# Edge columns of the filter loaded elsewhere, and small butterfly operations joined

## The chip, the cores and the metric

The kernel runs on one core of a Trainium2 chip. The metric is the device time of one execution in microseconds (us). The core's engines are TensorE (PE: matmuls; PEld its weight loads), VectorE (DVE), ScalarE (ACT), GpSimd (POOL) and SyncE (SP, which here only issues transfers); each runs its own list of instructions in order and waits for the others by semaphores. SP, ACT and POOL each have a queue of DMA transfers.

## The reference

```python
def _A_ref(x, w_r, w_i):
    X = jnp.fft.rfft2(x, axes=(-2, -1))
    X = X * (w_r + 1j * w_i)
    return jnp.fft.irfft2(X, s=(S, D), axes=(-2, -1))

def _B_ref(x, w1, w2):
    h = _silu(jnp.einsum("bsd,df->bsf", x, w1))
    return jnp.einsum("bsf,fd->bsd", h, w2)

xn = _layernorm(x, axis=-1)
s = _A_ref(xn, A_w_r, A_w_i)
g = _silu(_B_ref(xn, B_w1, B_w2))
return x + s * g
```

x is 2048 x 1024 (S x D), all in float32; w1 is 1024 x 3584, w2 3584 x 1024, and the filter w_r, w_i 2048 x 513 each.

## The kernel before

**Numbers.** Every operand of a matmul is split into a high and a low fp16 part, and a product is three matmuls (high-high, high-low, low-high). The high part is written by ACT (a copy with rounding), the low one by DVE (value minus high part, scalar_tensor_tensor at L230). The parts of the second matmul's operands travel through DRAM: hd_one, hd_sum and their like are stored on POOL's queue (L463) and loaded back as ht; w2's pieces are stored as ws and loaded back as jr (L387), then made into w by ACT (L227) and DVE (L230).

**The three streams of PE.** PE's list is written out ahead of time. First come 112 steps of the first matmul (h = xn w1, 24 matmuls of 128x512 each, L431). Then come 56 groups of the second matmul, pbM_J with M = 0 to 6 (seven products of a Strassen scheme over 2x2 blocks) and J = 0 to 7 (token tiles); a group is 42 matmuls (L509 to L511); the last one, pb6_7, is cut into two halves of half width. Between these stand, as a third stream in the background, the steps of the spectral part: layernorm, the forward transform (fa, then a butterfly on DVE at L757 to L790), the filter, the edge columns, and the inverse transform.

**The filter (f_gen, L883 to L1028)** runs in 16 steps u, beside the groups pb0_0 to pb2_x. A step loads vq (the forward result) and wq (four loads of the filter's columns) on SP's queue, multiplies on PE (fx, L914 to L916), forms X on DVE, scales wq on ACT (L997), multiplies X by wq on DVE (T, L1002), forms Z, and splits Z into the high and the low part of zq, in pieces by residue class (by_class, L937): ACT writes the high part (L954), DVE the low one (L960). Four steps fill one zq tile, which POOL's queue stores (zd, L965); the tile has a single buffer, so ACT's first piece of the next four waits for the stores. Each step also put two loads of the filter's edge columns (xsv, 64 x 4 elements of 4 bytes) on SP's queue (L987 to L989), delayed by a few steps (defer). edge_gen (L1030) uses them after the filter.

**The inverse transform (i_gen, L1122)** runs once per c, in the order 1, 3, 0, 2 (IORDER), beside groups pb2_x to pb6_x. At its start DVE copies the edge column into zt (L1129); PE's iu matmuls read zt. Then post (uw, ub, ud) and split make us on DVE and ACT, PE's id matmuls read us, and bfly (sw, st, spq, sab, so, s) makes the result s, which SP stores as sd. An output tile is the sum of a group's product and earlier ones (pl, kept), a silu on ACT (L590), and times s plus x on DVE (L583, L584), then a store.

**What sets the order.** While the list is written, `work()` (L1327) puts a background step behind a matmul step or group only while DVE's clock is not ahead of PE's by more than LEAD = 1:

```python
COST = {"DVE": ("dve", 0.07, 1.045e-3), "PE": ("pe", 0.0025, 0.4167e-3)}
...
clock["dve"] = max(clock["dve"], clock["pe"] - 1.0)
for _ in range(3):
    if clock["dve"] > clock["pe"] + LEAD or hold[0] or slot(bg) == PAUSE:
        break
```

Each DVE instruction moves DVE's clock by a fixed part and a part per element (meter, L189). So the number of DVE instructions decides where background steps stand on every engine's list.

Of the kernel before, what the change touches and what calls it, by code (L numbers as in the profile page):

```python
# [13 lines left out]
OP = mybir.AluOpType  # L14
# [90 lines left out]
def spectral_ffn(ctx, tc, x, w_r, w_i, w1, w2, ca, kc, ci, tw, pm, out):  # L105
# [648 lines left out]
    def fd_gen(c):  # L754
# [3 lines left out]
        def bfly(p):  # L758
# [12 lines left out]
            ds = ap.tile([128, 2, 2, 65], F32, name=f"DS{c}_{p}", tag="DS", bufs=1)  # L771
            tt(ds[:, 0], o[:, 1], o[:, 3], op=OP.subtract)
            tt(ds[:, 1], o[:, 1], o[:, 3], op=OP.add)
            pp = ap.tile([128, 4, 65], F32, name=f"P{c}_{p}", tag="P", bufs=1)
            tt(pp[:, 0:4:3], o[:, 0], o[:, 2, ::-1], op=OP.add)
            tt(pp[:, 2:0:-1], o[:, 0], o[:, 2, ::-1], op=OP.subtract)
            qq = ap.tile([128, 4, 65], F32, name=f"Q{c}_{p}", tag="Q", bufs=1)
            tt(qq[:, 0:4:3], ds[:, 0], ds[:, 1, ::-1], op=OP.add)
            tt(qq[:, 2:0:-1], ds[:, 0], ds[:, 1, ::-1], op=OP.subtract)
# [103 lines left out]
    def f_gen():  # L883
# [53 lines left out]
        def by_class(u):  # L937

            j = u % 4
            zv = zs_[u].rearrange("m n (i h l) -> m n h l i", h=2, l=8)  # L940
            qv = [zqs[u // 4][:, k].rearrange("m (n g b) i -> m n b g i", g=4, b=4)[:, :, :, :, 8 * j:8 * j + 8] for k in range(2)]
            first = [v[:, :, :, 0].rearrange("m n (l h) i -> m n h l i", h=2) for v in qv]
            for z, o in ((zv[:, :, :, 1:4], [v[:, :, 0:4:3, 3:0:-1] for v in qv]),
                         (zv[:, :, :, 5:8], [v[:, :, 2:0:-1, 1:4] for v in qv]),
                         (zv[:, :, :, 0:8:4], first)):
                yield z, o

        def high_z(u):
# [21 lines left out]
        for u in range(16):  # L970
# [56 lines left out]
        yield 1  # L1027

# [93 lines left out]
    def i_gen(c):  # L1122
# [21 lines left out]
        def post(g):  # L1144
# [4 lines left out]
            b = ip.tile([128, 2, 2, 128], F32, name=f"ub{c}_{g}", tag="ub", bufs=1)  # L1149
            d = ip.tile([128, 2, 2, 128], F32, name=f"ud{c}_{g}", tag="ud", bufs=1)  # L1150
# [37 lines left out]
        def bfly(p):  # L1188
# [110 lines left out]
    with tc.manual_schedule():  # L1299
# [79 lines left out]
        for n, (c, f) in enumerate(order):  # L1379
# [125 lines left out]
```

## Time and profile before

| what | us |
|---|---|
| median of 3 runs (1285.46, 1286.04, 1294.56) | 1286.04 |
| the profiled execution | 1284.65 |
| its span (first to last instruction) | 1282.9 |
| PE busy in it | 1234.2 (96%) |
| DVE busy | 1033.5 (81%) |
| ACT busy | 501.5 (39%) |
| POOL busy | 243.0 (19%) |

The span is the time from the first to the last instruction in the profiled execution; what lies around it is 1284.65 - 1282.9 = 1.75 us. TensorE's granted clock, as a mean over the span, was 0.985 of full speed. PE is the engine that is busy nearly throughout; the rows below tell where it is not. The lines of code are those of the kernel before.

### The profile page before, as it was taken

To read this page: it belongs to the slowest core of one execution; us is meant where nothing else is said; L and a number is where in the kernel's file an instruction comes from. 1 tells how busy PE (TensorE), PEld (TensorE's weight loads), DVE (VectorE), ACT (ScalarE), POOL (GpSimd) and SP (SyncE) were. 2 spreads that over 40 slices of the span, in tenths; PEclk is the share of its full clock that TensorE was granted. 3 is DMA by queue.
4 is the path that set the end of the run, shared out by engine and by line. 5 is a ranking of instruction groups with operands and counts; after the bars stand their busy time and mean duration, and the time that the engine had idled before them with its cause. 6 is when DMAs were issued, how large, how long until landed. Compare 5 with 4: busy or idle time off the path is not lost. (4 is left out here: it accounts for less than half of the span.)

```text
span 1282.9 us, 20862 instructions
## 1 busy us (share of the span) xinstructions
PE 1234.2 (96%) x7759; PEld 624.8 (49%) x7759; DVE 1033.5 (81%) x2284; ACT 501.5 (39%) x684; POOL 243.0 (19%) x389
## 2 busy tenths in 40 slices
PE   8998999999999999999999797999999998999996
PEld 5544455445445444445455454544554544455543
DVE  7688898998998997648957998872695896896897
ACT  4865344334365455436443443331122321332211
POOL 1231231222243344231221000013012010000000
PEclk9999999999999999999999798999999999999998
DMA  7477376565487779585876977877579599697688
GB/s 236 135 179 184 99 251 174 174 198 165 156 255 252 251 256 327 176 287 165 183 261 219 236 233 194 256 264 280 170 202 277 203 343 343 224 355 278 224 307 285
DMA packets 175735, 296.90 MB, mean 231 GB/s; under 512 B 39696, under 2 KB 92688, under 8 KB 175120
## 3 DMA queue, kind: packets, MB, share of 16 engines
q1 hardware_dynamic: 133232, 161.25, 41.1%
q0 software_dynamic: 26560, 82.86, 21.0%
q10 hardware_dynamic: 15840, 51.45, 11.6%
q8 instruction: 61, 1.00, 0.3%
q14 instruction: 42, 0.34, 0.1%
HBM read 186.97 MB, written 104.33 MB: 227 GB/s over the span
## 5 line engine op out<-in xcount | busy, mean ns | idle before, releaser
L431 PE MATMUL pa<-xnT,w 128*128 128x512 f16 x2688 | 586.7, 380 | 6.8 <-DMA xnT<-xs 4.4
L431 PEld LDWEIGHTS <-w 128*128 128x128 f16 x2688 | 262.6, 98 | 319.0 <-issue 7.7
L509 PE MATMUL pb<-w,ht 128*128 128x512 f16 (+1 forms) x798 | 301.6, 378 | 3.2 <-DMA ht<-hd_sum_d 3.2
L510 PE MATMUL pb<-w,ht 128*128 128x512 f16 (+1 forms) x798 | 301.0, 377 | 0.0
L511 PE MATMUL pb<-w,ht 128*128 128x512 f16 (+1 forms) x798 | 300.6, 377 | 0.0
L509 PEld LDWEIGHTS <-ht 128*128 128x128 f16 x798 | 78.4, 98 | 93.9 <-DMA ht<-hd_sum_d 3.4
L511 PEld LDWEIGHTS <-ht 128*128 128x128 f16 x798 | 78.4, 98 | 92.4 <-issue 2.1
L510 PEld LDWEIGHTS <-ht 128*128 128x128 f16 x798 | 78.4, 98 | 87.6 <-issue 1.3
L440 ACT ACTIVATE h<-pa,s 128x512 f32<-128x512 f32 x112 | 75.7, 676 | 104.2 <-PE pa L431 103.7
L227 ACT ACTIVATE w<-jr,sc 128x512 f16<-128x512 f32 x98 | 68.7, 713 | 108.0 <-DMA jr<-in_B_w_dram 82.2
L230 DVE SCALAR_TENSOR_TENSOR w<-jr,sc,w 128x512 f16<-128x512 f32 x98 | 71.6, 745 | 18.2 <-ACT w L227 18.2
L463 POOL DMA_DIRECT2D hd_sum<-hosum x52 | 38.0, 765 | 230.2 <-DVE hosum L230 115.2
L227 ACT ACTIVATE hoone<-h,hs 128x2048 f16<-128x2048 f32 x28 | 56.0, 1999 | 55.5 <-DMA hd_one<-hoone 26.0
L230 DVE SCALAR_TENSOR_TENSOR hoone<-h,hs,hoone 128x2048 f16<-128x2048 f32 x28 | 65.6, 2343 | 12.6 <-ACT hoone L227 12.6
L227 ACT ACTIVATE hosum<-hr,hs 128x1536 f16<-128x1536 f32 x28 | 44.0, 1572 | 76.5 <-DVE hr L470 61.3
L954 ACT ACTIVATE zq<-Z 128x192 f16<-128x192 f32 (+1 forms) x96 | 38.7, 483 | 79.3 <-DVE Z L217 58.9
L469 DVE TENSOR_TENSOR hr<-h 128x1024 f32<-128x1024 f32 x28 | 34.1, 1219 | 36.3 <-ACT h L440 36.2
L914 PE MATMUL fx<-vq,kq 128*128 128x256 f16 x192 | 47.8, 291 | 15.8 <-DMA vq<-vd 9.0
L463 POOL DMA_DIRECT2D hd_one<-hoone x52 | 45.2, 869 | 69.5 <-DVE hoone L230 24.2
L391 POOL DMA_DIRECT2D jr<-in_B_w_dram x28 | 24.6, 1018 | 171.1 <-DMA jr<-in_B_w_dram 35.3
L230 DVE SCALAR_TENSOR_TENSOR hosum<-hr,hs,hosum 128x1536 f16<-128x1536 f32 x28 | 50.7, 1810 | 4.7 <-ACT hosum L227 4.7
L227 ACT ACTIVATE w<-w1r,rs 128x1024 f16<-128x1024 f32 x28 | 32.0, 1145 | 49.8 <-DVE rs L258 22.4
(215 smaller groups left out, 1725.3 us busy)
## 6 DMA issues: line engine op xcount, KB each, us to landing
w1r<-in_B_w_dram SPq DMA_DIRECT2D x28, 512.0 KB, 5.8
w2m<-in_B_w_dram SPq DMA_DIRECT2D x28, 512.0 KB, 6.5
ht<-hd_dif ACTq DMA_DIRECT2D x32, 448.0 KB, 6.7
jr<-in_B_w_dram SPq DMA_DIRECT2D x56, 256.0 KB, 6.9
ht<-hd_sum ACTq DMA_DIRECT2D x32, 448.0 KB, 5.3
ht<-hd_one ACTq DMA_DIRECT2D x32, 448.0 KB, 6.7
hd_sum<-hosum POOLq DMA_DIRECT2D x52, 256.0 KB, 3.6
hd_one<-hoone POOLq DMA_DIRECT2D x52, 256.0 KB, 5.2
```

Of the source, the lines that this page charges most:

```text
L227: nc.scalar.activation(hi, raw, AF.Copy, scale=scale)
L230: nc.vector.scalar_tensor_tensor(lo, raw, scale, hi, op0=OP.mult, op1=OP.subtract)
L391: nc.gpsimd.dma_start(raw[n], w2_block(*todo[n], 1), accum_op=OP.add)
L431: nc.tensor.matmul(ps, w[:, wh, d], xt[:, xh, d], start=(n == 0), stop=(n == 23))
L440: nc.scalar.activation(hq[:, 2 * (c % 2) + f % 2], ps, AF.Silu, scale=s1[:, f:f + 1])
L463: defer(1, lambda k=k, m=m: stores[0].dma_start(hd[m, g][:, :, q].rearrange("f p h s -> f p (h s)"), o[:, k].rearrange("f p h s -> f p (h ...
L469: tt(sums[:, 0:2], hq[:, 0::2], hq[:, 1::2], op=OP.subtract)
L509: nc.tensor.matmul(ps, hh[:, 0], w[:, 0], start=first, stop=False)
L510: nc.tensor.matmul(ps, hh[:, 0], w[:, 1], start=False, stop=False)
L511: nc.tensor.matmul(ps, hh[:, 1], w[:, 0], start=False, stop=last)
L914: nc.tensor.matmul(o, k[:, c, kh, 1], v[:, c, vh], start=(n == 0), stop=False)
L954: nc.scalar.activation(o[0][:, :, h], z[:, :, h], AF.Copy)
```

## The change

In the filter, the two edge loads of each step leave SP's queue. A new function, load_edge, issues the same 32 loads on POOL's queue, one at each of the steps 44 to 75 of the first matmul. The classes of zq are written in five pieces in place of six, in another order of the 16 residues inside zq and zt. On DVE, operations on neighbouring tiles are written as one with a wider access pattern: in the forward butterfly P and Q are halves of one tile PQ, in post ub and ud halves of one tile, in bfly pairs of the last sums. DVE has 2062 instructions in place of 2286, ACT 752 in place of 768, SP 497 in place of 529, POOL 428 in place of 396. PE's are the same in number. The diff, cut to its core (bfly's first part and the common lines are left out):

```diff
@@ -768,15 +768,12 @@
...
-            ds = ap.tile([128, 2, 2, 65], F32, name=f"DS{c}_{p}", tag="DS", bufs=1)
-            tt(ds[:, 0], o[:, 1], o[:, 3], op=OP.subtract)
-            tt(ds[:, 1], o[:, 1], o[:, 3], op=OP.add)
-            pp = ap.tile([128, 4, 65], F32, name=f"P{c}_{p}", tag="P", bufs=1)
-            tt(pp[:, 0:4:3], o[:, 0], o[:, 2, ::-1], op=OP.add)
-            tt(pp[:, 2:0:-1], o[:, 0], o[:, 2, ::-1], op=OP.subtract)
-            qq = ap.tile([128, 4, 65], F32, name=f"Q{c}_{p}", tag="Q", bufs=1)
-            tt(qq[:, 0:4:3], ds[:, 0], ds[:, 1, ::-1], op=OP.add)
-            tt(qq[:, 2:0:-1], ds[:, 0], ds[:, 1, ::-1], op=OP.subtract)
+            tt(t0[:, 0], o[:, 1], o[:, 3], op=OP.subtract)
+            tt(t0[:, 1], o[:, 1], o[:, 3], op=OP.add)
+            pq = ap.tile([128, 2, 4, 65], F32, name=f"PQ{c}_{p}", tag="PQ", bufs=1)
+            pp, qq = pq[:, 0], pq[:, 1]
+            tt(pq[:, :, 0:4:3], t0[:, 4::-4], t0[:, 6::-5, ::-1], op=OP.add)
+            tt(pq[:, :, 2:0:-1], t0[:, 4::-4], t0[:, 6::-5, ::-1], op=OP.subtract)
...
@@ -937,27 +934,24 @@
...
-            zv = zs_[u].rearrange("m n (i h l) -> m n h l i", h=2, l=8)
-            qv = [zqs[u // 4][:, k].rearrange("m (n g b) i -> m n b g i", g=4, b=4)[:, :, :, :, 8 * j:8 * j + 8] for k in range(2)]
-            first = [v[:, :, :, 0].rearrange("m n (l h) i -> m n h l i", h=2) for v in qv]
-            for z, o in ((zv[:, :, :, 1:4], [v[:, :, 0:4:3, 3:0:-1] for v in qv]),
-                         (zv[:, :, :, 5:8], [v[:, :, 2:0:-1, 1:4] for v in qv]),
-                         (zv[:, :, :, 0:8:4], first)):
-                yield z, o
+            zv = zs_[u].rearrange("m n (i l) -> m n l i", l=16)
+            qv = [zqs[u // 4][:, k].rearrange("m (n l) i -> m n l i", l=16)[:, :, :, 8 * j:8 * j + 8] for k in range(2)]
+            for first, n, to, by in ((1, 3, 0, 4), (4, 4, 14, -4), (9, 4, 3, 4), (13, 3, 9, -4)):
+                stop = to + by * (n - 1) + (1 if by > 0 else -1)
+                yield zv[:, :, first:first + n], [v[:, :, to:stop if stop >= 0 else None:by] for v in qv]
+            yield zv[:, :, 0:9:8], [v[:, :, 12:14] for v in qv]
...
             for z, o in by_class(u):
-                for h in range(2):
-                    nc.scalar.activation(o[0][:, :, h], z[:, :, h], AF.Copy)
+                nc.scalar.activation(o[0], z, AF.Copy)
...
             for z, o in by_class(u):
-                for h in range(2):
-                    nc.vector.tensor_tensor(o[1][:, :, h], z[:, :, h], o[0][:, :, h], op=OP.subtract)
+                nc.vector.tensor_tensor(o[1], z, o[0], op=OP.subtract)
...
@@ -984,9 +978,6 @@
...
-            i_, n_, q_ = u // 8, u // 4 % 2, u % 4
-            for b in range(2):
-                defer(3, lambda i_=i_, n_=n_, q_=q_, b=b: nc.sync.dma_start(xsv[64 * b:64 * b + 64, 1 + n_, q_, :, i_:i_ + 1], wv[i_][q_][b, :, :, 512 * n_:512 * n_ + 1]))
...
@@ -1026,6 +1017,11 @@
...
+    def load_edge(k):
+        n_, b, q_ = k // 4 % 2, k // 8 % 2, k % 4
+        i_ = k // 16
+        nc.gpsimd.dma_start(xsv[64 * b:64 * b + 64, 1 + n_, q_, :, i_:i_ + 1], wv[i_][q_][b, :, :, 512 * n_:512 * n_ + 1])
...
@@ -1126,7 +1122,7 @@
...
-        nc.vector.tensor_copy(zt[:, :, :, :, 0, 0], zp[:, c])
+        nc.vector.tensor_copy(zt[:, :, :, :, 12, 0], zp[:, c])
...
@@ -1136,7 +1132,7 @@
...
-                            lhs = zt[rows_, q, zh, r, 4 * g:4 * g + 4].rearrange("m l i -> m (l i)")
+                            lhs = zt[rows_, q, zh, r, 12 - 4 * g:16 - 4 * g].rearrange("m l i -> m (l i)")
...
@@ -1146,22 +1142,20 @@
...
-            b = ip.tile([128, 2, 2, 128], F32, name=f"ub{c}_{g}", tag="ub", bufs=1)
-            d = ip.tile([128, 2, 2, 128], F32, name=f"ud{c}_{g}", tag="ud", bufs=1)
+            bd = ip.tile([128, 2, 2, 2, 128], F32, name=f"ub{c}_{g}", tag="ub", bufs=1)
+            b, d = bd[:, 0], bd[:, 1, :, ::-1]
...
-            tt(bv[:, 0], sums[:, 0:2], sums[:, 2:4], op=OP.add)
-            tt(dv[:, 0], sums[:, 0:2], sums[:, 2:4], op=OP.subtract)
-            for j, x_, y_ in ((0, dif[:, 0], dif[:, 2, ::-1]), (1, turn[:, 0:2, 0], turn[:, 2:4, 0])):
-                tt(bv[:, 1, j, 0], x_[:, 0], y_[:, 0], op=OP.subtract)
-                tt(dv[:, 1, j, 1], x_[:, 1], y_[:, 1], op=OP.subtract)
-                tt(dv[:, 1, j, 0], x_[:, 0], y_[:, 0], op=OP.add)
-                tt(bv[:, 1, j, 1], x_[:, 1], y_[:, 1], op=OP.add)
...
+            tt(b[:, :, :, 0:64], sums[:, 0:2], sums[:, 2:4], op=OP.add)
+            tt(d[:, :, :, 0:64], sums[:, 0:2], sums[:, 2:4], op=OP.subtract)
+            x_ = w[:, 1:3, 0].rearrange("m j k a -> m k j a")
+            y_ = w[:, 1:3, 2, ::-1].rearrange("m j k a -> m k j a")
+            tt(bd[:, :, :, 0, 64:128], x_, y_, op=OP.subtract)
+            tt(bd[:, ::-1, :, 1, 64:128], x_, y_, op=OP.add)
...
@@ -1210,21 +1204,16 @@
...
-            tt(s_[:, 0], pc, u, op=OP.add)
-            tt(s_[:, 4], pc, u, op=OP.subtract)
-            tt(s_[:, 2], pm_, v, op=OP.subtract)
-            tt(s_[:, 6], pm_, v, op=OP.add)
-            stt(s_[:, 1], o12[:, 0], RH, qm, op0=OP.mult, op1=OP.add)
-            stt(s_[:, 5], o12[:, 0], -RH, qm, op0=OP.mult, op1=OP.add)
-            stt(s_[:, 7], o12[:, 1], RH, qp, op0=OP.mult, op1=OP.add)
-            stt(s_[:, 3], o12[:, 1], -RH, qp, op0=OP.mult, op1=OP.add)
+            tt(s_[:, 0:7:6], pq[:, :, 0], ab[:, :, 0], op=OP.add)
+            tt(s_[:, 4:1:-2], pq[:, :, 0], ab[:, :, 0], op=OP.subtract)
+            stt(s_[:, 1:8:6], o12, RH, pq[:, ::-1, 1], op0=OP.mult, op1=OP.add)
+            stt(s_[:, 5:2:-2], o12, -RH, pq[:, ::-1, 1], op0=OP.mult, op1=OP.add)
...
@@ -1398,6 +1387,8 @@
...
             chunks[0] = sum(last_use[k] < n for k in range(4))
+            if 44 <= n < 76:
+                load_edge(n - 44)
...
```

The order of the lists moves with the count. Three places follow. The first is SP's queue in the filter stage, around the load of vq8. Of the kernel before (jr28 is a piece of w2, wq7 the filter's columns for step 7):

```order
L387 DMA jr27_6652<-ws1_13_164 128x512
L387 DMA jr28_6726<-ws2_0_165 128x512
L387 DMA jr29_6736<-ws2_1_166 128x512
L989 DMA xsv_215<-in_A_w_r_dram 64x4x1 x2
L902 DMA wq7_0_6770<-in_A_w_r_dram 64x4x128 x2
L902 DMA wq7_1_6773<-in_A_w_i_dram 64x4x128 x2
L387 DMA jr30_6776<-ws2_2_167 128x512
L894 DMA vq8_6787<-vd0_75 128x2048
```

Of the changed kernel:

```order
L387 DMA jr27_6601<-ws1_13_164 128x512
L387 DMA jr28_6680<-ws2_0_165 128x512
L891 DMA vq8_6691<-vd0_75 128x2048
L387 DMA jr29_6707<-ws2_1_166 128x512
L899 DMA wq7_0_6739<-in_A_w_r_dram 64x4x128 x2
L899 DMA wq7_1_6742<-in_A_w_i_dram 64x4x128 x2
L387 DMA jr30_6745<-ws2_2_167 128x512
```

The edge loads are gone, and vq8 stands behind jr28, where before it stood behind jr30.

The second is DVE's list where the inverse transform of c = 0 begins (zt0 is the copy that PE's iu0 waits for; pl4_3 and pl4_4 are the additions behind the groups pb4_3 and pb4_4; w2_5 is a low part of w2's pieces). Before:

```order
L557 TENSOR_TENSOR pl4_3_1_10787<-pl4_3_1_10787,pb4_3_10761 128x512
L558 TENSOR_TENSOR pl4_3_0_10789<-pl4_3_0_10789,pb4_3_10761 128x512
L230 SCALAR_TENSOR_TENSOR w2_5_1_10645<-jr83_10716,sc2_228,w2_5_1_10645 128x512
L583 SCALAR_TENSOR_TENSOR pl4_3_1_10787<-fs1_3_0_10819,s_sc_218,pl4_3_1_10787 128x512
L584 TENSOR_TENSOR pl4_3_1_10787<-pl4_3_1_10787,fx1_3_0_10821 128x512
L557 TENSOR_TENSOR pl4_4_1_10863<-pl4_4_1_10863,pb4_4_10837 128x512
L558 TENSOR_TENSOR pl4_4_0_10865<-pl4_4_0_10865,pb4_4_10837 128x512
L1129 COPY zt0_10199<-zp_214 128x16
L1151 TENSOR_TENSOR uw0_0_11057<-iu0_0_10959,uw0_0_11057 128x512
```

Changed:

```order
L557 TENSOR_TENSOR pl4_3_1_10596<-pl4_3_1_10596,pb4_3_10570 128x512
L558 TENSOR_TENSOR pl4_3_0_10598<-pl4_3_0_10598,pb4_3_10570 128x512
L230 SCALAR_TENSOR_TENSOR w2_5_1_10485<-jr83_10556,sc2_228,w2_5_1_10485 128x512
L1125 COPY zt0_10000<-zp_214 128x16
L1147 TENSOR_TENSOR uw0_0_10803<-iu0_0_10705,uw0_0_10803 128x512
```

The copy moved up, from behind the additions of group pb4_4 to behind the w2 piece that follows those of pb4_3. On PE's list iu0 moved from behind pb4_5 to behind pb4_4; iu3 likewise moved from the middle of pb3_5 to behind pb3_4 (its copy from behind the kept addition of group 4 to the w2 piece behind that of group 3), iu2 from behind pb5_6 to behind pb5_5, id3 from the middle of pb4_0 to behind pb3_7, id0 from behind pb5_1 to the middle of pb5_0, and id2 from the middle of pb6_2 to behind pb6_0.

The third is DVE's list at the end, from the last instruction of the last butterfly (s2_3). Before:

```order
L1227 SCALAR_TENSOR_TENSOR s2_3_13193<-so2_3_13192,spq2_3_13186 128x128
L583 SCALAR_TENSOR_TENSOR pl6_3_2_12985<-fs0_3_1_13013,s_sc_218,pl6_3_2_12985 128x512
L584 TENSOR_TENSOR pl6_3_2_12985<-pl6_3_2_12985,fx0_3_1_13015 128x512
L583 SCALAR_TENSOR_TENSOR pl6_3_0_12987<-fs0_3_0_13017,s_sc_218,pl6_3_0_12987 128x512
L584 TENSOR_TENSOR pl6_3_0_12987<-pl6_3_0_12987,fx0_3_0_13019 128x512
L569 TENSOR_TENSOR pl6_4_2_13135<-pl6_4_2_13135,pb6_4_13107 128x512
L570 TENSOR_TENSOR pl6_4_0_13137<-pl6_4_0_13137,pb6_4_13107 128x512
```

Changed:

```order
L1216 SCALAR_TENSOR_TENSOR s2_3_12771<-so2_3_12770,spq2_3_12764 128x2x128
L583 SCALAR_TENSOR_TENSOR pl6_1_2_12494<-fs0_1_1_12596,s_sc_218,pl6_1_2_12494 128x512
L584 TENSOR_TENSOR pl6_1_2_12494<-pl6_1_2_12494,fx0_1_1_12598 128x512
L583 SCALAR_TENSOR_TENSOR pl6_1_0_12496<-fs0_1_0_12600,s_sc_218,pl6_1_0_12496 128x512
L584 TENSOR_TENSOR pl6_1_0_12496<-pl6_1_0_12496,fx0_1_0_12602 128x512
L569 TENSOR_TENSOR pl6_2_2_12714<-pl6_2_2_12714,pb6_2_12686 128x512
L570 TENSOR_TENSOR pl6_2_0_12716<-pl6_2_0_12716,pb6_2_12686 128x512
```

The last butterfly now ends ahead of the outputs of group pb6_1; before it ended ahead of those of pb6_3.

## Rows read from the trace of the kernel before

**Rows 1.** The page, part 1: busy time, share and instructions.

```profile
PE 1234.2 (96%) x7759; PEld 624.8 (49%) x7759; DVE 1033.5 (81%) x2284; ACT 501.5 (39%) x684; POOL 243.0 (19%) x389
```

**Rows 2.** PE's waits: engine, line, releaser: us in total, times, longest.

```profile
PE fx L914 <- DMA vq<-vd: 9.0, 1, 9.0
PE fx L914 <- DMA jr<-ws: 6.8, 1, 6.8
...
PE pb L509 <- DMA ht<-hd_sum_d: 3.2, 1, 3.2
```

**Rows 3.** Stretches: length, busy of PE, PEld, DVE, ACT, POOL, clock, DMA, GB/s.

```profile
240.00:400.00 160.00, 160.00 (x873) 78.27 (x872) 150.83 (x313) 73.02 (x86) 49.17 (x69) 1.00 0.66 207
690.00:860.00 170.00, 149.37 (x879) 81.01 (x877) 150.41 (x292) 68.80 (x140) 11.09 (x26) 0.93 0.81 238
```

**Rows 4.** The same table for two short stretches.

```profile
719.00:729.00 10.00, 5.63 (x38) 4.65 (x39) 9.93 (x19) 3.00 (x8) 0.00 (x0) 0.50 0.90 291
1080.00:1086.00 6.00, 3.23 (x99) 2.90 (x100) 1.79 (x4) 1.32 (x2) 0.00 (x0) 1.00 0.91 301
```

**Rows 5.** Timelines of SP, ACT and DVE, 676 to 692 us: start, length, work, idle.

```profile
676.53 1.27 SPq L989 DMA_DIRECT2D xsv<-in_A_w_r_dram  x2
677.89 4.22 SPq L902 DMA_DIRECT2D wq<-in_A_w_r_dram  x2
...
689.02 0.72 ACT L227 ACTIVATE w<-jr,sc 128x512 f16<-128x512 f32 x1 [8.04 <-DMA wq<-in_A_w_r_dram]
...
681.22 2.17 DVE L960 TENSOR_TENSOR zq<-Z,zq 128x192 f16<-128x192 f32 x6
690.39 1.22 DVE L1002 TENSOR_TENSOR T<-X,wq 128x1024 f32<-128x1024 f32 x1 [7.00 <-ACT wq L997]
```

**Rows 6.** Waits of ACT and of DVE, 655 to 860 us.

```profile
ACT zq L954 <- DMA zd<-zq: 20.4, 3, 10.5
...
DVE T L1002 <- ACT wq L997: 14.0, 6, 7.0
```

**Rows 7.** Timeline of DVE in a last butterfly, 1130 to 1132 us.

```profile
1130.36 0.21 DVE L1200 SCALAR_TENSOR_TENSOR sw<-sw,st 128x64 f32<-128x64 f32 x1
1130.49 0.21 DVE L1201 SCALAR_TENSOR_TENSOR sw<-sw,st 128x64 f32<-128x64 f32 x1
...
1131.15 0.42 DVE L1210 TENSOR_TENSOR spq<-sw 128x256 f32<-128x256 f32 x1
1131.49 0.42 DVE L1211 TENSOR_TENSOR spq<-sw 128x256 f32<-128x256 f32 x1
```

**Rows 8.** The page, part 5: a group of instructions on POOL.

```profile
L463 POOL DMA_DIRECT2D hd_sum<-hosum x52 | 38.0, 765 | 230.2 <-DVE hosum L230 115.2
```

**Rows 9.** Timelines of PE and DVE around two starts of the inverse transform (iu).

```profile
983.66 0.38 PE L510 MATMUL pb<-w,ht 128*128 128x512 f16 x1
...
989.70 0.38 PE L511 MATMUL pb<-w,ht 128*128 128x512 f16 x1
...
1082.77 0.40 PE L1141 MATMUL iu<-kk,zt 64*128 64x128 f16 x8 [3.55 <-DVE zt L1129]
...
989.85 0.20 DVE L1129 COPY zt<-zp 128x16 f16<-128x16 f16 x1
...
1075.57 0.75 DVE L230 SCALAR_TENSOR_TENSOR w<-jr,sc,w 128x512 f16<-128x512 f32 x1 [1.37 <-ACT w L227]
...
1081.91 0.69 DVE L558 TENSOR_TENSOR pl<-pl,pb 128x512 f32<-128x512 f32 x1 [2.61 <-DMA pl<-pd]
```

**Rows 10.** Timelines of PE, SP and DVE at the end.

```profile
1270.33 0.27 PE L511 MATMUL pb<-w,ht 128*128 128x256 f16 x1
...
1267.20 0.32 SPq L502 DMA_DIRECT2D pl<-pd  x1
...
1271.83 0.42 DVE L569 TENSOR_TENSOR pl<-pl,pb 128x256 f32<-128x256 f32 x1 [4.63 <-DMA fs<-sd]
...
1277.21 0.41 DVE L569 TENSOR_TENSOR pl<-pl,pb 128x256 f32<-128x256 f32 x1
```

More of the change, by code (lines that the diff above doesn't have):

```diff
@@ L1154, in post @@
             nc.vector.tensor_single_scalar(dif[:, 1:4:2], dif[:, 1:4:2], RH, op=OP.mult)
-            tt(turn[:, 0:4:3, 0], dif[:, 1:4:2, 0], dif[:, 1:4:2, 1], op=OP.subtract)
-            tt(turn[:, 1:3, 0], dif[:, 1:4:2, 0], dif[:, 1:4:2, 1], op=OP.add)
-            bv, dv = (v.rearrange("m c r (e a) -> m e c r a", e=2) for v in (b, d))
-            tt(bv[:, 0], sums[:, 0:2], sums[:, 2:4], op=OP.add)
-            tt(dv[:, 0], sums[:, 0:2], sums[:, 2:4], op=OP.subtract)
-            for j, x_, y_ in ((0, dif[:, 0], dif[:, 2, ::-1]), (1, turn[:, 0:2, 0], turn[:, 2:4, 0])):
-                tt(bv[:, 1, j, 0], x_[:, 0], y_[:, 0], op=OP.subtract)
-                tt(dv[:, 1, j, 1], x_[:, 1], y_[:, 1], op=OP.subtract)
-                tt(dv[:, 1, j, 0], x_[:, 0], y_[:, 0], op=OP.add)
-                tt(bv[:, 1, j, 1], x_[:, 1], y_[:, 1], op=OP.add)
+            tt(turn[:, 0:3:2, 0], dif[:, 1:4:2, 0], dif[:, 1:4:2, 1], op=OP.subtract)
+            tt(turn[:, 0:3:2, 1], dif[:, 1:4:2, 0], dif[:, 1:4:2, 1], op=OP.add)
+            tt(b[:, :, :, 0:64], sums[:, 0:2], sums[:, 2:4], op=OP.add)
[4 more added lines that the diff above has]
+            tt(bd[:, ::-1, :, 1, 64:128], x_, y_, op=OP.add)
             u = ip.tile([128, 8, 128], F32, name=f"uu{c}_{g}", tag="s", bufs=2)
@@ L1199, in bfly @@
             stt(o1[:, 0], d1[:, 1], -S16, t_[:, 2, 0], op0=OP.mult, op1=OP.add)
-            stt(o1[:, 1], d1[:, 0], S16, t_[:, 2, 1], op0=OP.mult, op1=OP.add)
+            wd, wo, tf = (v.rearrange("s g r d -> s (g r) d") for v in (w[:, 1], w[:, 2], t_))
+            stt(wo[:, 3:8:4], wd[:, 3:7:3], S16, tf[:, 0:6:5], op0=OP.mult, op1=OP.add)
             stt(o3[:, 0], d3[:, 0], S16, t_[:, 0, 1], op0=OP.mult, op1=OP.subtract)
-            stt(o3[:, 1], d3[:, 1], S16, t_[:, 0, 0], op0=OP.mult, op1=OP.add)
             tt(o2[:, 0], t_[:, 1, 0], t_[:, 1, 1], op=OP.subtract)
@@ L1212, in bfly @@
             tt(abv[:, 0], y1, y3, op=OP.add)
-            tt(abv[:, 1], y1, y3, op=OP.subtract)
-            pc, qp, pm_, qm = pq[:, 0, 0], pq[:, 0, 1], pq[:, 1, 0], pq[:, 1, 1]
-            u, t_, r, v = ab[:, 0, 0], ab[:, 0, 1], ab[:, 1, 0], ab[:, 1, 1]
+            tt(abv[:, 1, ::-1], y1, y3, op=OP.subtract)
+            t_, r = ab[:, 0, 1], ab[:, 1, 1]
             o12 = ip.tile([128, 2, 128], F32, name=f"so{c}_{p}", tag="so", bufs=1)
```

## The prediction

> **What bounds the kernel now.** I read the engines' shares first. TensorE (PE) is busy 1234.2 of 1282.9 us [rows 1], so a faster VectorE (DVE) pays only where PE waits for it, and behind PE's last matmul. Next the list of PE's waits: 9.0 + 6.8 us stand at the filter's matmuls (fx) and 3.2 us at the second matmul's operand (ht) [rows 2]; the inverse transform's (iu) stands under [rows 9]. Then the table of stretches: in 690 to 860 us PE works 149.37 of 170 us, idle 20.6, at a mean granted clock of 0.93, while DVE is busy 150.41 [rows 3]. The clock comes on top of each stall: from 719 to 729 us, around the second stall, PE's 5.63 busy us ran at 0.50, the lower of its two levels [rows 4], 2.8 us lost; at the stage's mean of 0.93 the loss is at most 0.07 x 149 = 10.5 us. So this stage holds up to 31 us, and the end another 12.3: the last matmul begins at 1270.33 us and lasts 0.27 [rows 10], and the span ends at 1282.9. The rest of PE's time is matmuls, whose number the change leaves alone.
>
> **The DVE instructions.** It removes 224 of DVE's 2286 instructions and no element: 32 in the forward butterfly, 96 in the inverse one, 80 in the last (sw), 16 in the filter's classes. The price of one is read from starts: operations of 64 elements follow each other every 0.135 us, of 256 every 0.34 [rows 7]; the slope is 0.205/192 = 1.07 ns an element, and 0.135 - 64 x 0.00107 = 0.067 us is left for the instruction. 224 x 0.067 = 15 us of DVE. Most lies beside PE work and is worth nothing by itself; per inverse butterfly pair (a post and a sw) it is 11 x 0.067 = 0.74 us. The new operands keep runs of 64 or 65 contiguous elements, so I keep that slope. The filter's pieces do not: their inputs stand 64 bytes apart, as before. Six pieces, of 171 elements on the mean, take 2.17 us [rows 5], 0.36 each or 2.1 ns an element, so five save one instruction, 0.07 us a step, 1.1 us in all. The Trainium skill (SBUF — State Buffer, the note on cachelines) says that consecutive accesses pay when each falls into a new 16-byte line; the longer time per element of these pieces agrees with it, and by it joining them cannot bring the 1.07 ns.
>
> **The edge loads.** 32 loads of 64x4x1 elements leave SP's queue in the filter stage. A pair costs SP 1.27 us [rows 5], 16 pairs 20 us. The place that shows most: such a pair was issued at 676.53 us, and the next two filter loads (wq) then took SP 4.22 us; ACT stood 8.0 us for these loads, and DVE, with nothing else to do, 7.00 until 690.39 [rows 5]. That idle stretch ends in PE's ht and fx stalls some 15 to 30 us later. In 655 to 860 us DVE waits 14.0 us for ACT's scaling of wq [rows 6], 7.0 of it here. With the pair gone, and step 8's operand (vq8) in the queue ahead of the w2 pieces 29 and 30 and of four wq loads that it stood behind, I take that 7.00 as gained. Gains stop there: ACT also waits 20.4 us, three times, for the zq stores (single buffer), the longest 10.5 [rows 6], and stores are not made faster; and DVE's own work fills 88% of the stage. PE gets no more than DVE's chain gains. Bounds: 2 us, if the stores take back what is gained; 16, if all of DVE's 14.0 and its 1.1 return, with a us of clock. Inside I take **-7**, by the one pair that the trace shows.
>
> On POOL's queue the loads come one for each of 32 first-matmul steps, at about 235 to 400 us. POOL is busy 49.17 of 160 us in 240 to 400 [rows 3]; a store's issue there costs 0.765 us [rows 8], so 24 us more; even at twice that POOL stays below its 160. PE is busy 160.00 of those 160 us [rows 3], and each store waits at most one load longer. I cost this at **0**; the cover is that the edge values are read only at the end of the filter stage and the hd stores have 300 us. If the cover fails, ACT waits for hd buffers and PE for ACT. The Trainium skill (DMA: Bandwidth & Descriptors, SWDGE vs HWDGE vs iDMA) says that GpSimd writes its descriptors into rings in SBUF that DVE locks it out of in its 2-port mode, and that SP's DMAs are immune: by it this move goes the wrong way. The trace doesn't bear it out at this size: with DVE busy 150.83 of 160 us the stores' mean issue is 0.765 us [rows 3, 8].
>
> **The order that moves.** The planner meters DVE by instruction, so cheaper butterflies put inverse steps earlier on PE's list. Their condition, the zt copy on DVE, moves less. iu3 comes half a group earlier, and a group is 42 matmuls, whose starts lie 0.216 us apart (28 steps from 983.66 to 989.70), 9.1 us: PE asks at 985.4 rather than right after the matmul at 989.70. The copy, at 989.85 behind group 4's addition, loses only that one addition of 0.6 us [rows 9]; it would come at 989.2 and, with DVE running earlier, about 1.3 sooner. New stall 2.5, within 0 to 3.8: **+2.5**. iu0 comes a whole group earlier, 1070 rather than 1079; the copy moves from behind group 4's addition, which waited for a transfer (1081.91), to behind group 3's and one w piece (1075.57 + 0.7) [rows 9]. Stall 6.2 instead of 3.55: **+2.6**, between -3.5 (w comes early) and +5.5. Of the clock I add 0.4 for both: the stall before iu0 cost none, since the granted clock stood at 1.00 through 1080 to 1086 [rows 4].
>
> **The end.** The last butterfly (sw of tile 3) moves from behind group 6_3 to behind 6_1, two groups earlier, and DVE has only output work behind it. Before, that butterfly and the outputs queued behind it kept the pl loads of the last group, whose buffers come free late, from being issued until 1267.20, and its addition waited 4.63 us, to 1271.83 [rows 10]. Without the backlog the first half of the last group is ready at about 1266.0 (4.6 us of its 42 half-width matmuls before 1270.6), its addition and the outputs of groups 6_6 and 6_7a take 5.4 us (1271.83 to 1277.21 [rows 10]), PE's last half is done at 1270.6 and the closing chain, from the addition at 1277.21 to the end, is 5.7 long [rows 10]: 1266.0 + 5.4 + 5.7 = 1277.1. **-5.8**; 3 if the loads stay half as late, 6.6 if the half waits for PE alone.
>
> **Sum.** -7 + 2.5 + 2.6 + 0.4 - 5.8 = -7.3, and a group of small items (the ht stall and the matmuls of the edges) at -1: -8.3. From the profiled execution's 1284.65 us that is 1276.3, and from the median, 1.4 higher, 1277.7; in between I say **1276.5**. A measurement here can tell about 1% (12.9 us), so faster means below 1273.2, slower above 1298.9.
>
> **Rivals.**
> A. *SP's queue was the whole cause.* For: DVE's six waits for wq, and PE's two fx stalls both name loads [rows 2, 6]. Against: the zq stores. Both fx stalls, the ht and edge stalls go (20.6 us) and half the clock loss (5); then -25.6 + 5.5 - 5.8 = -26, **1258.5**. Chance 0.15. Between A and the forecast, with two of the 14.0's larger waits gone (-12) and the iu stalls filled, 1284.65 - 12 - 5.8 + 1 = **1268**: 0.22.
> B. *The stores set the filter's pace.* Then -2 there, +5.5, -3 at the end: **1285**, no change. For: 10.5 us in one wait. Against: the tail gains by itself. Chance 0.16.
> C. *Steps asked for too early, slower.* iu3, iu0, iu2 and id2 each come 4.5 to 9.1 us sooner; if no zt copy or us tile comes sooner, PE's queue stands for it, as it stands 3.55 us at iu0 now [rows 9]. It decides from the point at which the four stalls pass the 13 us won elsewhere: 3.8 + 6.2 + 9.1 + 9.1 less the 3.55 now is 24.7, with half of the 2.8 us of [rows 4] for each 30: 1284.65 + 30 - 12.8 = **1302**. Against: group-5 additions ended in time for iu2 and id2 by my arithmetic. Over 1298.9 0.04; the edge loads holding back hd stores share it.
> D. *The joins don't join.* Had the joined operations the rate of the filter's pieces, 2.1 ns an element, DVE would lose more than the 15 us it saves; the end would gain only by its order, -3, filter as forecast: **1280**. Chance 0.07.
>
> **Chances.** Forecast 0.36, A 0.15, between 0.22, B 0.16, D 0.07, C 0.04. Faster: A, the case between, and of the forecast's the lower few per cent: 0.40. Slower 0.04; same 0.56. The range from 1261 to 1288 leaves out most of A's lower half and C, with a little beyond B: 2 in 10. The forecast's own is 1270 to 1283.
>
> **What would show it.** Right: no 7 us idle of DVE before the multiplication (T) at some 690 us; wq pairs at 1.3 us on SP throughout; PE idle in 690 to 860 down by some 5 to 9 us; waits of PE at iu3 and iu0 of 2 and 6 us; 6 to 7 us from the last matmul to the end. Wrong: fx stalls as long as before behind zq's stores (B), fx stalls gone (A), a wait at iu2 or id2 of over 4 us (C), joined operations of 128 elements above 0.3 us (D), or PE idle in 240 to 400 us (POOL).

## The result: 0.4% slower, and the profile after

The changed kernel takes 1290.51 us (median of 20 runs, 1286.16 to 1293.04); the kernel before took 1284.67 beside it (20 runs). The ratio is 1.0042, 95% interval [1.0028, 1.0056]: slower by some 5.4 us, where 1276.5, a gain of 8 to 10, had been forecast. The profiled execution has a span of 1290.6 us at a mean granted clock of 0.979.

The page's part 1 of the kernel after:

```profile
PE 1239.9 (96%) x7759; PEld 630.9 (49%) x7759; DVE 1020.4 (79%) x2060; ACT 500.2 (39%) x668; POOL 264.2 (20%) x421
```

DVE is busy 13 us less than in [rows 1], where 15 were counted; PE is busy 5.7 us *more* with the same matmuls, which is the granted clock. PE's list of waits (engine, line, releaser: us in total, times, longest) tells where:

```profile
PE fx L911 <- DMA vq<-vd: 13.0, 2, 8.7
PE iu L1137 <- DVE zt L1125: 11.5, 2, 8.3
PE eps L1047 <- POOL edge L1040: 4.3, 1, 4.3
```

Of [rows 2] the two fx waits became 13.0 us from 15.8, and ht's is 2.2, from 3.2. The edge's matmul (eps) waits 4.3 us, where before it waited 1.6, and iu, at which PE had waited 3.55 us once [rows 9], waits 11.5 in two waits. The table of stretches (as [rows 3, 4]; the last number but two is the clock):

```profile
240.00:400.00 160.00, 160.00 (x891) 79.06 (x890) 153.04 (x313) 75.62 (x89) 64.03 (x92) 1.00 0.65 204
690.00:860.00 170.00, 150.19 (x883) 82.42 (x882) 143.98 (x274) 64.73 (x124) 11.06 (x26) 0.93 0.80 239
852.00:862.00 10.00, 6.98 (x26) 5.03 (x27) 2.97 (x5) 2.50 (x5) 4.36 (x16) 0.60 0.97 358
988.00:998.00 10.00, 7.74 (x112) 5.85 (x113) 5.92 (x16) 1.79 (x3) 1.73 (x2) 0.83 0.96 260
1076.00:1094.00 18.00, 9.73 (x119) 6.91 (x117) 9.81 (x22) 3.56 (x5) 0.88 (x1) 0.72 0.94 308
```

PE still has no idle time in 240 to 400 us, though POOL is busy 15 us more there. In 690 to 860 DVE works 6.4 us less and PE gains 0.8. The three short stretches are those behind the waits at eps, iu3 and iu0: the clock is 0.60, 0.83 and 0.72.

The end answers to [rows 10] (timelines of PE, SP and DVE):

```profile
1283.17 0.27 PE L511 MATMUL pb<-w,ht 128*128 128x256 f16 x1
...
1274.75 0.99 SPq L502 DMA_DIRECT2D pl<-pd  x2
...
1279.49 0.42 DVE L569 TENSOR_TENSOR pl<-pl,pb 128x256 f32<-128x256 f32 x1 [3.90 <-DMA pl<-pd]
...
1284.87 0.41 DVE L569 TENSOR_TENSOR pl<-pl,pb 128x256 f32<-128x256 f32 x1
```

From the end of the last matmul to the end of the span it is 7.2 us now, 12.3 before: the last group's addition still waits, 3.90 us in place of 4.63, but it now begins 3.7 us ahead of the last matmul, where before it began 1.5 behind it.

Cut at the first fx matmul, the first iu matmul and the end of the last matmul, the profiled executions divide so (us; the stretch ahead of the first fx took 579 to 581 us in every kernel but the one with small stores, where it took 592, and is not shown):

| kernel | median, ratio to before [95%] | filter: fx to iu | iu to last matmul | end |
|---|---|---|---|---|
| before | 1283 to 1285 | 326.4 | 365.1 | 12.3 |
| changed | 1290.51, 1.0042 [1.0028, 1.0056] | 326.3 | 376.5 | 7.2 |
| edge loads alone on POOL | 1286.72, 1.0022 [1.0004, 1.0040] | 326.8 | 366.9 | 12.6 |
| no edge loads | 1286.31, 1.0014 [1.0000, 1.0027] | 326.8 | 364.4 | 12.5 |
| joins, edge loads on SP | 1289.00, 1.0037 [1.0019, 1.0055] | 321.9 | 375.0 | 6.5 |
| changed, order of before | 1283.03, 0.9989 [0.9970, 1.0008] | 327.1 | 365.2 | 9.1 |
| changed, early zt copies | 1281.37, 0.9971 [0.9952, 0.9989] | 325.8 | 366.3 | 7.2 |
| the same, edge loads on SP | 1282.99, 0.9988 [0.9970, 1.0005] | 326.9 | 367.3 | 7.2 |
| small zq stores | 1279.89, 0.9954 [0.9932, 0.9976] | 308.9 | 368.0 | 13.2 |
| both mends | 1272.39, 0.9900 [0.9880, 0.9919] | 316.2 | 366.6 | 7.1 |
| both mends, no joins | 1278.58, 0.9946 [0.9924, 0.9968] | 317.8 | 369.4 | 12.9 |
| both mends, zq in halves | 1267.33, 0.9856 [0.9830, 0.9883] | 309.6 | 367.9 | 7.1 |

Between the first two rows: nothing in the filter as a whole, +11.4 us in the inverse transform's stretch, -5.1 at the end (and 1.6 ahead of the first fx, within what that stretch differs by among all the kernels). Executions of one kernel differ by up to 14 us, so a stretch of one profile is read to some 3 to 5 us, and the ratios decide.

### The profile page after: what moved, and what is told of

It reads as the page before. It is cut to its first block, busy times and chain, and to the rows that moved or that the text cites. A ratio compares the mean times of both kernels' runs of the same rounds, so it can differ in the third digit from the quotient of the medians.

```text
span 1290.6 us, 20649 instructions
## 1 busy us (share of the span) xinstructions
PE 1239.9 (96%) x7759; PEld 630.9 (49%) x7759; DVE 1020.4 (79%) x2060; ACT 500.2 (39%) x668; POOL 264.2 (20%) x421
## 5 line engine op out<-in xcount | busy, mean ns | idle before, releaser
L949 ACT ACTIVATE zq<-Z 128x192 f16<-128x192 f32 (+2 forms) x80 | 37.2, 543 | 106.8 <-DVE Z L217 70.0
L230 DVE SCALAR_TENSOR_TENSOR hoone<-h,hs,hoone 128x2048 f16<-128x2048 f32 x28 | 65.6, 2343 | 10.8 <-ACT hoone L227 10.8
L911 PE MATMUL fx<-vq,kq 128*128 128x256 f16 x192 | 47.3, 289 | 13.3 <-DMA vq<-vd 13.0
```

Source lines behind the costliest of these rows:

```text
L230: nc.vector.scalar_tensor_tensor(lo, raw, scale, hi, op0=OP.mult, op1=OP.subtract)
L911: nc.tensor.matmul(o, k[:, c, kh, 1], v[:, c, vh], start=(n == 0), stop=False)
L949: nc.scalar.activation(o[0], z, AF.Copy)
```

## The experiments

**The edge loads alone** (before, with load_edge and its call, and without the loads on SP):

> The kernel before with the edge loads alone moved to POOL's queue; no DVE instruction and no place on PE's list changes. Theory (the gain of SP is swallowed by the zq stores that the next zq tile waits for, and the whole loss comes from the order that the joined operations bring): -3 to 0 us against before, DVE's 7.0 us wait at some 690 us gone and ACT's wait for the zq stores longer by about as much. Rival 1 (the loads on POOL cost: they hold hd stores, or contend with DVE for the descriptors): +3 to +6 us. My recorded forecast: -7.

Ratio 1.0022, +2.8 us: between the theory's -3 to 0 and the +3 to +6 of rival 1. The interval (+0.5 to +5.1 us) reaches into the rival's range and just misses the theory's. PE's waits at fx are 16.7 us, at eps 5.3.

**No edge loads at all** (the output's edge part is left out):

```diff
-            for b in range(2):
-                defer(3, ... nc.sync.dma_start(xsv[...], wv[i_][q_][...]))
+                if not q:
+                    nc.gpsimd.memset(xsv[:, 1:3], 0.0)
```

> The kernel before without any loads of the filter's edge columns (they are set to zero once; the output's edge part is left out). Theory (SP's 20 us of edge loads held nothing up in the end, because the next zq tile waits for its stores anyway): -1 to +3 us against before, like the kernel with the edge loads on POOL, PE's waits in the filter stage still 18 us or more together. Rival 1 (moving them to POOL is what cost the 2.8 us): faster than before by 3 us or more, so 5 or more faster than with the loads on POOL. Recorded forecast: -7.

1.0014, as with the loads on POOL within the intervals: taking the edge loads (25.8 us of SP's queue in all, where the prediction had 20 from one pair) off SP gains nothing in the total, wherever they go, and rival 1, by which it would be 3 us or more faster than before, is out. The waits of ACT and DVE in 655 to 860 us of this kernel show why (in total, times, longest):

```profile
ACT zq L954 <- DMA zd<-zq: 35.2, 3, 13.8
...
DVE w L230 <- ACT w L227: 13.2, 2, 7.4
DVE zq L960 <- ACT zq L954: 9.9, 3, 5.6
...
DVE T L1001 <- ACT wq L996: 2.5, 2, 1.7
```

In [rows 6] DVE waited 14.0 us for ACT's wq and ACT 20.4 for the zq stores. Now it is 2.5 and 35.2, and DVE waits behind ACT at w and zq, 23.1 us, where it had waited 10.8. Most of what SP gave, the stores took; what became of the rest stands with the filter below.

**The zq stores cut** (on the kernel with the edge loads alone; most of the filter's result is left out):

```diff
-                    defer(1, lambda c=c: stores[0].dma_start(zd[c][:, q], zv[:, :, c]))
+                    r_ = 128 if q == 3 else 8
+                    defer(1, lambda c=c, r_=r_: stores[0].dma_start(zd[c][0:r_, q], zv[0:r_, :, c]))
...
```

> The kernel with only the edge loads moved, and the zq stores of the first three of four tiles cut to 8 of 128 rows (the rows left out hold constants stored during the first matmul; so most of the filter's result is left out of the inverse transform). Theory (the stores set the pace once SP is free): ACT's three waits for the stores (20 us or more) shrink to under 3, and with them PE's waits in the filter stage fall by 8 to 15 us: -8 to -14 us against the kernel with the edge loads alone. Rival 4 (DVE's own work or the loads of vq and wq set the pace): within 3 us of it.

The ratio is 0.0068 below that kernel's, -8.7 us, though the constants' stores cost 11 us in the first matmul (the start of fx moved from 581 to 592); the filter stage fell by 17.9 us, more than forecast. ACT's waits for the stores and PE's waits at fx in it:

```profile
ACT zq L954 <- DMA zd<-zq: 15.0, 2, 7.8
...
PE fx L914 <- DVE w L230: 5.8, 1, 5.8
...
PE fx L914 <- DMA vq<-vd: 2.7, 1, 2.7
```

PE waits 8.5 us at fx, where it was 16.7, and not at ht or eps. ACT's waits fell from 35.7 to 15.0 and not under 3: small stores too land late in that stretch. So the stores bear on the filter's pace. How much of the 17.9 us comes from the later start of fx instead is open; zq in halves, below, tells the stores' part without it.

**The joins alone** (the changed kernel with the edge loads back on SP):

> The changed kernel with its edge loads back on SP's queue in the filter stage: joins, five pieces, and the changed kernel's order on PE. Theory (order): +5 to +8 us against before, as the whole change, with waits of PE at iu3 of 2 to 4 us and at iu0 of 6 to 9 us. Rival 1 (edge loads on POOL cost): 0 to +2. Recorded forecast for this part: 0 to -1 (stalls at iu against the end).

+4.7 us, close to the whole change, and PE waits at iu as there:

```profile
PE iu L1135 <- DVE zt L1123: 10.0, 2, 8.1
```

Its filter is 4.4 us shorter in this profile: PE came to eps 4.3 us later than in the changed kernel, when POOL's first copy was just done, and lost nothing there. With early zt copies the same exchange of queues gives 326.9 against 325.8, and the profiled execution (1285.31 us) is 3.7 below this kernel's median, so I take that for the spread of single executions.

**The order of before, with the joins:**

```diff
+            clock["dve"] += 2 * 0.07
...
+            clock["dve"] += 0.07
...
+            clock["dve"] += 6 * 0.07
...
+            clock["dve"] += 5 * 0.07
```

The four lines stand behind the forward butterfly, the zq pieces, post and the last butterfly.

> The changed kernel, but the planner is charged 0.07 us for each DVE instruction that the joins took away, so that PE's and SP's lists stand in the order of before (without the edge loads on SP). Theory (order): no wait at iu3, 0 to 3.5 us at iu0, -1 to -5 us against before, since DVE has 15 us less to do and the end has less in front. Rival 2 (the joined operations or the new layout of zq and zt themselves cost time): +3 us or more.

-1.4 us, 7 less than the changed kernel: the same instructions on the same engines, only later on PE's list. PE's matmuls stand in the order of before. Its waits at iu (1.97 us at iu3, where none was expected, and 0.55 at iu0):

```profile
PE iu L1139 <- DVE zt L1127: 2.5, 2, 2.0
PE iu L1139 <- DVE uw L1150: 1.6, 1, 1.6
```

So neither the joined operations nor the new layout cost the 3 us of rival 2. The end is 9.1 us: part of its gain is DVE's shorter work, the rest is order.

**Early zt copies** (the order of the changed kernel, three 0.2 us copies some three DVE instructions earlier):

```diff
...
+        for n_ in range(4 if c != IORDER[0] else 0):
+            if n_ == 1:
+                was = clock["dve"]
+                nc.vector.tensor_copy(zt[:, :, :, :, 12, 0], zp[:, c])
+                late, clock["dve"] = clock["dve"] - was, was
+            yield PAUSE
...
```

> The changed kernel, all lists alike but for three small copies: the edge column is copied into zt3, zt0 and zt2 three planner steps earlier on DVE, ahead of three w2 pieces or so and of the addition of the group before. Theory (PE waits at iu3 and iu0 because the copy stands in DVE's list behind w2 pieces that wait for their loads): both waits (3.3 and 8.3 us) under 1 us, some 15 us with the granted clock less than the changed kernel, so -8 to -11 us against before. Rival 3 (the stall only moves: PE then waits as long at the next product, or for ht, or the end grows by what PE gains): -3 us to +3 us against before.

-9.1 us against the changed kernel, -3.7 against before. The orders of PE's matmuls and of SP's queue are the changed kernel's, and no wait for zt is left. It is less than forecast, in part since PE, past the copy, waits 3.7 us for DVE to read iu's PSUM (uw):

```profile
PE eps L1047 <- POOL edge L1040: 3.8, 1, 3.8
PE iu L1143 <- DVE uw L1154: 3.7, 2, 2.4
```

So the order on PE was not what cost; three copies were in the wrong place for it. **With the edge loads on SP** instead:

> Joins, five pieces, early zt copies, but the edge loads on SP's queue as before. Theory (it does not matter for the filter's end on which queue the edge loads stand): within 2.5 us of the kernel with the early zt copies, -2 to -6 us against before. Rival 1 (POOL is the wrong queue for them): 3 us or more faster than that kernel.

0.9988 against 0.9971, within the intervals and as the theory had it.

**Both mends.** The last loss of the filter stage is at eps: POOL issues the last four zq stores first (2.8 us), which wait for DVE's last zq pieces, and only then makes the twelve small copies that eps reads. Here these copies stand in front (edge_copies, taken out of edge_gen); nothing moves on PE's and SP's lists.

```diff
+        edge_copies()
         high_z(15)
         yield 1
...
```

> The kernel with the early zt copies, and POOL's twelve small copies for the edge columns ahead of the last four zq stores on POOL's list, where they stood behind them. Theory (PE's 4 us at the edge's matmul come from POOL issuing the stores first, 2.8 us, behind DVE's last zq pieces; what the filter stage gains at PE is lost there, and the clock falls behind it): the wait of 3.8 us goes, and up to 4 us of low clock after it: -4 to -8 us against the kernel with the early zt copies, -8 to -11 against before. Rival (PE then waits as long for the next thing, ACT's copy of the edge or POOL's sums): within 2 us.

1272.39 us, ratio 0.9900: 9 us less than with the early copies alone, above the forecast. The wait was 3.8 us, and the clock behind it as much again. The stretch 852 to 862 us, with the early copies alone:

```profile
852.00:862.00 10.00, 9.52 (x32) 5.93 (x33) 0.75 (x1) 2.19 (x4) 2.28 (x16) 0.50 1.02 369
```

and with both mends:

```profile
852.00:862.00 10.00, 10.00 (x48) 4.52 (x47) 1.67 (x3) 0.72 (x1) 1.17 (x7) 1.00 1.02 371
```

9.52 busy us at 0.50 against 10.00 at 1.00: 4.8 us of matmul time, beside the wait. From the first eps matmul to the first iu it is 47.3 us, and was 52.1. PE no longer waits at eps; it still waits 12.7 us at fx, 4.2 at iu (for uw) and 2.0 at ht.

**Both mends without the joins:**

> Both mends and the edge loads on POOL's queue, without the joins and the five pieces: before's order on PE. Theory (once no copy stands in the way, what the joins bring is the end of the kernel, 5 us, and little else): 3 to 6 us slower than the kernel with both mends and the joins, so -7 to -10 us against before. Rival 2 (the joins cost somewhere, or bring nothing): within 2 us of it.

0.9946 against 0.9900: once nothing stands in the way, the joins bring 5.9 us (some 2 to 10 by the two intervals); in the profiles 5.8 of the difference is at the end (12.9 against 7.1). The same run tells something of the edge loads: its filter takes 317.8 us, 9.0 less than with the edge loads alone on POOL, and differs from it by the two mends.

**zq in halves:**

```diff
-                zqs[q] = bp.tile([128, 2, 128, 32], F16, name=f"zq{q}", tag="zq", bufs=1)
+                zqs[q] = [bp.tile([128, 1, 128, 32], F16, name=f"z{k}q{q}", tag=f"z{k}q", bufs=1) for k in "hl"]
...
+            if j == 3:
+                put(q, 0)
...
```

put(q, 0) issues the four stores of the high half, behind ACT's last piece.

> The kernel with both mends (early zt copies, edge copies ahead of the stores), and zq cut into a tile of high and a tile of low parts, with stores of their own: the high parts go out as soon as ACT has written them, some 4 us before DVE ends the low ones, so that ACT's next high piece waits less. No work is left out. Theory (the zq stores set the filter's pace): ACT's three waits for stores fall from 35 us together by 3 to 4 us each, the filter stage by 3 to 8 us, -3 to -8 us against the kernel with both mends. Rival (POOL's 8 issues in place of 4, and more transfers at once in a full DMA stretch, eat it): within 2 us, or slower.

ACT waits for the stores once, 8.8 us, in place of 35.4 in three waits, and the filter falls to 309.6 us from 316.2:

```profile
ACT zhq L954 <- DMA zd<-zhq: 8.8, 1, 8.8
```

1267.33 us, by the ratios 5.6 us less than with both mends, as forecast: the stores did hold the filter back. It is 1.4% below before and 1.9% below the changed kernel: the version that beats both, with no work left out.

## Why the prediction was wrong

**The filter, -7: nothing.** The first half held: the 7.00 us of DVE at 690 [rows 5] are gone. DVE's T starts at 684.94, and the step runs on until it meets the stores (timelines of ACT before, then of the changed kernel ACT, DVE and POOL):

```profile
699.92 0.53 ACT L954 ACTIVATE zq<-Z 128x192 f16<-128x192 f32 x1 [7.86 <-DMA zd<-zq]
```

```profile
699.83 0.52 ACT L949 ACTIVATE zq<-Z 128x192 f16<-128x192 f32 x1 [14.00 <-DMA zd<-zq]
```

```profile
684.94 1.23 DVE L993 TENSOR_TENSOR T<-X,wq 128x1024 f32<-128x1024 f32 x1
...
694.41 0.74 DVE L230 SCALAR_TENSOR_TENSOR w<-jr,sc,w 128x512 f16<-128x512 f32 x1
702.77 0.75 DVE L230 SCALAR_TENSOR_TENSOR w<-jr,sc,w 128x512 f16<-128x512 f32 x1 [7.61 <-ACT w L227]
```

```profile
685.57 2.85 POOL L959 DMA_DIRECT2D zd<-zq  x4 [3.20 <-ACT w L227]
```

ACT's next zq piece begins at 699.83 us; before it was 699.92. The stores were issued from 685.57 and had landed 14 us later, in a stretch where the DMA engines had no idle share (the last number but one):

```profile
686.00:700.00 14.00, 14.00 (x110) 8.68 (x108) 9.09 (x18) 0.17 (x1) 2.42 (x4) 1.00 1.03 361
```

DVE stands 7.61 us, where it had stood 7.00 twelve us earlier. For the whole stage (ACT, then DVE):

```profile
ACT zq L949 <- DMA zd<-zq: 36.8, 3, 14.0
...
DVE w L230 <- ACT w L227: 13.4, 2, 7.6
DVE zq L954 <- ACT zq L949: 9.8, 3, 5.7
DVE T L993 <- ACT wq L988: 3.5, 3, 1.5
```

I had [rows 6] with 20.4 us of ACT waiting for these stores in front of me and wrote that they were not made faster; but I put them down as a bound (2 us, rival B at 0.16) and took the gain of the one pair as the value. A wait of 7.86 us that ACT already had at 699.92 could only grow by what came sooner. The step that failed is "I take that 7.00 as gained".

Some of it did come through, and was lost at the edge's matmul. Counted from the first fx, PE is ready for eps at 270.0 us, 5.6 sooner than before (275.6); with the edge loads alone on POOL or left out it is 270.3. But eps reads POOL's copies (edge), and these stand behind the last four zq stores, which wait for DVE's last zq piece (POOL and PE, before):

```profile
853.25 2.84 POOL L965 DMA_DIRECT2D zd<-zq  x4 [49.18 <-DVE zq L960]
...
856.36 0.40 PE L1051 MATMUL eps<-edge,perm 128*128 128x24 f32 x2 [1.61 <-POOL edge L1044]
```

Changed:

```profile
851.93 2.82 POOL L959 DMA_DIRECT2D zd<-zq  x4 [50.28 <-DVE zq L954]
...
855.02 0.62 PE L1047 MATMUL eps<-edge,perm 128*128 128x24 f32 x2 [4.29 <-POOL edge L1040]
```

Counted from the first fx again, these stores come only 2.9 us sooner (271.2 for 274.1): that is what DVE's chain, the joins' shorter work included, kept of the 7.00 behind the stores of the tiles before (1.6 and 1.5 without the joins, in the kernels with the edge loads alone moved or left out). So PE's wait grows by 2.7 us, and the clock takes 2.8 more: from eps to the first iu it is 52.0 us for 49.1, and 47.3 in the four kernels where PE does not wait there. -5.6 + 2.7 + 2.8 is the nothing that was measured. The prediction had the matmuls of the edges among its small items at -1. The sizes are those of single profiles, but the six others with the loads off SP's queue and zq stored whole come to eps at 268.9 to 270.5, but for one at 273.4, and the two others with them on it at 271.9 and 274.3. No run has the edge copies in front with the loads still on SP: by its own 1.6 us of wait and 1.8 of clock, before would have won an estimated 3.4.

**The order, +2.5 and +2.6: +11.4 together with the clock.** At iu3 (DVE, PE):

```profile
988.74 0.69 DVE L553 TENSOR_TENSOR kept<-kept,pb 128x512 f32<-128x512 f32 x1 [3.87 <-ACT c L552]
989.34 0.75 DVE L230 SCALAR_TENSOR_TENSOR w<-jr,sc,w 128x512 f16<-128x512 f32 x1
990.01 0.20 DVE L1125 COPY zt<-zp 128x16 f16<-128x16 f16 x1
...
990.26 4.48 PE L1137 MATMUL iu<-kk,zt 64*128 64x128 f16 x96 [3.25 <-DVE zt L1125]
```

The stall is 3.25 us (forecast 2.5). The c that the addition waited for stood on ACT's list behind a w piece, which waited for its w2 load until 987.25:

```profile
987.25 0.72 ACT L227 ACTIVATE w<-jr,sc 128x512 f16<-128x512 f32 x1 [3.16 <-DMA jr<-in_B_w_dram]
```

At iu0 (ACT, DVE, PE):

```profile
1083.07 0.72 ACT L227 ACTIVATE w<-jr,sc 128x512 f16<-128x512 f32 x1 [4.16 <-DMA jr<-in_B_w_dram]
...
1083.82 0.75 DVE L230 SCALAR_TENSOR_TENSOR w<-jr,sc,w 128x512 f16<-128x512 f32 x1 [1.55 <-ACT w L227]
1084.49 0.20 DVE L1125 COPY zt<-zp 128x16 f16<-128x16 f16 x1
...
1084.75 5.15 PE L1137 MATMUL iu<-kk,zt 64*128 64x128 f16 x96 [8.27 <-DVE zt L1125]
```

8.27 us (forecast 6.2): the w piece in front of the copy ended its wait for a w2 load at 1083.07, two us later against PE than I had carried over from before. The larger miss is the clock: I charged 0.4 us, because the one such stall in the trace, 3.55 us, cost none [rows 4]. The two runs of iu matmuls behind the copies now last 4.48 and 5.15 us, where the same 96 of iu0 took 2.85 before:

```profile
1082.77 2.85 PE L1141 MATMUL iu<-kk,zt 64*128 64x128 f16 x96 [3.55 <-DVE zt L1129]
```

That is 3.9 us. So 3.25 + (8.27 - 3.55) + 3.9 = 11.9, of the 11.4 seen. The terms that failed are the 0.4 for the clock and, less, the stall at iu0. Rival C named this mechanism and priced it. iu2 and id2, half of its price, did stay clear, so it did not come to its 1302; but I gave it a chance only for passing the 1%, and left its smaller sizes out.

**The end, -5.8: -5.1.** The size was right, and the last loads do come earlier against PE, as named (the row of before names a load of fs for the 4.63 us, the changed one the load of pl that was meant). But the prediction put the gain down to the move of the last butterfly: the joined kernel in the order of before, with an end of 9.1 us, shows that some 3 of the 5 come from DVE's shorter work alone.

**The joins, 0.067 us each.** Right; a joined operation of two times 128 elements (timeline of DVE) follows the next in 0.34 us, as [rows 7] had it for 256, so rival D is out:

```profile
1132.54 0.42 DVE L1213 TENSOR_TENSOR s<-spq,sab 128x256 f32<-128x256 f32 x1
1132.88 0.42 DVE L1214 TENSOR_TENSOR s<-spq,sab 128x256 f32<-128x256 f32 x1
```

A zq piece of 256 elements takes 0.580 us (line 954, us in total and mean ns), 2.3 ns an element for the 2.1 of the prediction, so its price per element stayed, and five pieces bring no more than the one instruction:

```profile
L954 DVE TENSOR_TENSOR zq<-Z,zq 128x256 f16<-128x256 f32 x32 | 17.3, 580 | 0.1
```

**The edge loads on POOL, 0.** Right as to POOL: they took 0.88 to 0.97 us each, the stores' mean went from 0.765 to 0.769 [rows 8], and PE did not wait in that stretch:

```profile
L463 POOL DMA_DIRECT2D hd_sum<-hosum x52 | 38.1, 769 | 230.9 <-DVE hosum L230 90.1 <-issue 41.6 <-ACT h L440 24.4
...
L1023 POOL DMA_DIRECT2D xsv<-in_A_w_i_dram x16 | 13.3, 879 | 1.3 <-DMA xsv<-in_A_w_i_dram 1.0 <-DMA hd_sum_d<-hosum 0.4
L1023 POOL DMA_DIRECT2D xsv<-in_A_w_r_dram x16 | 13.3, 971 | 0.0
```

The Trainium skill (DMA: Bandwidth & Descriptors, SWDGE vs HWDGE vs iDMA) ties the lock between DVE and POOL's descriptors to DVE's 2-port mode; no row tells how much of DVE's 153.04 busy us is in it, and none shows a cost. The same page (Issuing engines are not separate DMA queues) says that another issuing engine saves only the time to issue, since all transfers run on the same engines. That agrees: PE is ready for eps as soon with the loads on POOL's queue as without any (270.3 us from the first fx).

**The sum.** -7 and the small -1 became 0, +5.5 became +11.4, and the end fell 0.7 short: 1276.5 and what failed, 7 + 1 + 5.9 + 0.7, make 1291.1, where 1290.51 was measured.

## What to carry to other kernels

A wait that is removed pays only up to the next resource with a wait in the same step: ask what was already late behind it, and take that as the value, not as a bound. Follow the gain to the last thing that the stage hands on, too: here POOL's copies for eps kept PE from what the steps ahead had won. Where a planner sets the order by cost, cheaper work moves its consumers forward, and a small operation that gates them has to move as well: ahead of everything on its engine that waits for a transfer. On PE a stall is counted with the matmuls behind it, where the clock falls: they ran at 0.50 until it was granted again.

## What the runs showed of the hardware

A wait of PE of 3.55 us had no price in clock at iu0 before (1.00 through 1080 to 1086), 1.6 us behind one of 3.25 at iu3, and 4.8 us behind one of 3.8 at eps; a wait of only 1.61 at eps before cost 1.8. So the length of the wait does not tell the price, and these runs leave open what does. And the four zq stores of 512 KB each took up to 15 us to land with the DMA engines full, where their issue cost POOL 2.85 us: in the kernel with halved tiles, issuing half of the bytes as soon as ACT had written them was worth 5 to 6 us.
